# Decayed linear attention and two MLPs: the order of a chunk's attention products, old state first instead of alternating by pairs of heads

## The chip, the core and the metric

The kernel runs on one core of one Trainium2 chip. The metric is the device time of one execution in microseconds (us). Three executions of the kernel before took 604.82, 605.13 and 610.63 us; the median is 605.13.

## What is computed

Attention over 2 batches, 8 heads, 768 tokens and 64 features a head, with a decay per head instead of a softmax, and then two MLPs of 512 to 2048 to 512 on the 1536 tokens. The reference, cut:

```python
for b in range(nb):                                        # attention, block by block
    intra = einsum('bhic,bhjc->bhij', qb, kb) * Dmask      # scores, decayed and causal
    intra = einsum('bhij,bhjd->bhid', intra, vb)           # values
    inter = einsum('bhid,bhde->bhie', qb * lam_pow, kv_state)   # old state
    out[:, :, sl] = intra + inter
    kv_state = lam_block * kv_state + einsum('bhsd,bhse->bhde', kb * rev_pow, vb)
h = x @ w_in;  x = (h * clip(h + 3, 0, 6) / 6) @ w_out     # first MLP
h = relu(x @ w_in2);  out = (h * h) @ w_out2               # second MLP
```

## The kernel before

The attention is done in 12 chunks of 128 tokens, 6 for each batch. The MLPs work on three blocks of 4 chunks (512 tokens). All products are float32. The weights arrive as float64 and are turned into two float32r parts each ("decoding", lines 144 to 191) mostly on VectorE, 64 pieces of 512 numbers a partition. Decoding steps are handed out by `fill` and `weight` between the other steps of VectorE.

For one chunk the attention has these parts; the names are those of the tiles in the trace.

- Scores (`scores`, L286): `psc`, keys by queries, for the first block with a block diagonal query (L295, full array), for later chunks one product for each head with 64 rows (L305). The eight heads of a chunk lie in two PSUM tiles, one for each half t of the rows. VectorE multiplies them with the decay into `A` (L299, L307).
- New state (`state_values`, L316): `pst`, eight products of the decayed keys `kd` and the values, 128 rows by 64 columns of the array. VectorE makes the new state `kv` of it and of `kvs`, the old state decayed by GpSimd (L323, L326). The last chunk of a batch (5 and 11) has none.
- The chunk's output (`state_values`): `px` in this text, `pxt` in the trace, one PSUM tile. To every head belong an old-state product (L334: 64 rows by 64 columns, of `kv_old` and the decayed query `qs`) and a values product (L337: 128 rows by 64 columns, of `v` and `A`), which is added to it. The first chunk of a batch (0 and 6) has no old state. ScalarE copies the sum into `xh` (L339) and VectorE takes the rest into `xl` (L342).
- GpSimd makes `kd` and `qs` for the next chunk in `prepare` (L272, L280, L282). `kd` and `qs` have one buffer each, so `qs` of the next chunk can be made only when the last old-state product of this chunk has read the buffer, and `kd` when the last new-state product has.

An old-state or values product of one head (64 by 128 outputs in float32) stands in the trace as two matmul records; so eight products are a group of 16 records. The words F, S, N, O and V stand below for the big products of the MLPs (`ph` L358, `py` L395), the scores of later chunks, the new state, the old state and the values.

Chunks 0 to 3 are done first, with seven PSUM buffers (the stage up to 34.4 us). From there on chunks 4 to 11 are spread through the first MLP's work, and all their PSUM tiles (`psc` twice, `pst`, `pxt`) share a pool `ps_a` of two buffers, handed out in turn: scores take both, then the two tiles of `state_values`, then the next scores. A tile waits until the tile two places before it has been read. The order on every engine is set by a scheduler that may put big products between the parts of a chunk; TensorE then runs its list in that order and waits at the first instruction that isn't ready. The attention ends at 107 us; nothing behind it differs.

Of the kernel before, what the change touches and what calls it, by code (L numbers as in the profile page):

```python
# [8 lines left out]
F32 = mybir.dt.float32  # L9
# [5 lines left out]
ALU = mybir.AluOpType  # L15
PSUM = bass.MemoryType.PSUM

P = 128
BLOCKS = (4, 4, 4)  # token blocks, in chunks of 128
WBUFS = {"wi": 5, "wo": 7}  # chunks of weights held as hi and lo  # L20
WARM = 10
RAW = 4  # loads of weights under way
GROUP = 4  # chunks of 128 hidden units that are summed in PSUM
# us of decoding given to VectorE after each part of a unit of work
FILL = {"s": 0.8, "h1": 1.0, "h2": 0.8, "y": 1.6, "a": 1.0}


# [1 line left out]
def decay_attention_moe_moe(  # L29
# [10 lines left out]
    w_out2: bass.AP,  # L40
    out: bass.AP,
):
    """Decayed linear attention and two MLPs.

    The weights are float64, given as int64 of the same bits. A weight, and every other
    operand of the large products, is held as the sum of two float32r numbers (hi of 12
    significant bits and lo of the rest); hi*hi + hi*lo + lo*hi has float32's accuracy.
    Activations stay transposed, [feature, token], up to the last product.

    lam: [128, head] the same in every row, then [head of a pair (64 rows each), pair]  # L50
    qT, kT: [chunk of 128 tokens, (head of a pair, feature), (pair, token)]
    k, v: [chunk, token, (head, feature)]
    w_in: [chunk of 128 hidden units, feature in its chunk, (chunk of features, unit, word)]
    w_out: [chunk of 128 hidden units, unit, (feature, word)]
    """
    nc = tc.nc
    NC = qT.shape[0]
    NP = lam.shape[1] // 3
    H = 2 * NP
    D = k.shape[2] // H  # L60
# [13 lines left out]

    halves = [slice(D * t, D * (t + 1)) for t in range(2)]

    # ---------------------------------------------------------------- loads
    # The first block's chunks borrow the sums' place; their queries lie block diagonal, so
    # that their products fill the array and bring TensorE's clock up.
    kT_t, k_t, q_t, v_t = {}, {}, {}, {}  # L80
    n_first = min(BLOCKS[0], 4)

# [27 lines left out]
        nc.sync.dma_start(out=k_t[c], in_=k[c])  # L110
        nc.sync.dma_start(out=v_t[c], in_=v[c])

    # ------------------------------------------------------- float64 weights
    keys = []
    n_ahead = WBUFS["wo"] - GROUP
    for i in range(2 * NF // GROUP):
# [4 lines left out]
        keys += [("wo", *x) for x in (fs[n_ahead:] if i else fs)]  # L121
    n_loaded, n_begun = 0, 0
    raw_t, abs_t, w_t = {}, {}, {}
    n_done = {"wi": 0, "wo": 0}  # weights that have had their last use
    pieces = []

    def load_ahead(n):
# [7 lines left out]
            n_loaded += 1  # L135

    def magnitude(n):
        """The exponent's lower eight bits become float32's."""
        if n < len(keys) and n not in abs_t:
            load_ahead(n + 1)  # L140
            abs_t[n] = dec.tile([P, DM], F32, tag="a", name="da")
            nc.scalar.activation(abs_t[n], raw_t[n][:, :, 1].bitcast(F32), AF.Abs, scale=2.0**16)  # L142

    def decode_steps(n):
        """Turns 512 float64 of every partition into hi and lo."""
        key = keys[n]
        kind = key[0]
        magnitude(n)
        t, a = raw_t.pop(n), abs_t.pop(n)
        lo32, hi32 = t[:, :, 0], t[:, :, 1]  # L150
        ai = a.bitcast(I32)
        u = dec.tile([P, DM], I32, tag="u", name="du")
        hi = wsp.tile([P, DM], F32R, tag=kind + "h", name=kind + "h", bufs=WBUFS[kind])
        lo = wsp.tile([P, DM], F32R, tag=kind + "l", name=kind + "l", bufs=WBUFS[kind])

        def clamp():
            # Under 2^-126: 0; from 2^128: inf.
            nc.vector.tensor_scalar(a, a, 2.0, 1.875 * 2.0**32, op0=ALU.max, op1=ALU.min)
            magnitude(n + 1)

        def shift():
            nc.vector.tensor_scalar(
                ai, ai, 4, 1, op0=ALU.logical_shift_left, op1=ALU.logical_shift_right
            )

        def join():
            # u: the value cut to 21 significant bits.
            nc.vector.scalar_tensor_tensor(  # L168
                u, hi32, -(2**31), ai, op0=ALU.bitwise_and, op1=ALU.bitwise_or
            )  # L170
            nc.scalar.copy(hi, u.bitcast(F32))  # L171

        def power():
            # a: sign and power of two.
            nc.vector.tensor_scalar(ai, u, -(2**23), None, op0=ALU.bitwise_and)

        def lower():
            # a: what the lower word stands for.
            nc.vector.scalar_tensor_tensor(  # L179
                a, lo32.bitcast(U32), 2.0**-52, a, op0=ALU.mult, op1=ALU.mult  # L180
            )

        def rest():
            nc.vector.tensor_tensor(u.bitcast(F32), u.bitcast(F32), hi.bitcast(F32), op=ALU.subtract)  # L184

        def add():
            nc.vector.tensor_tensor(lo, u.bitcast(F32), a, op=ALU.add)  # L187
            w_t[key] = (hi, lo)
            load_ahead(n + 1 + RAW)

        return [(0.34, clamp), (0.34, shift), (0.6, join), (0.34, power), (0.6, lower), (0.6, rest), (0.6, add)]
# [28 lines left out]
            assert decode_piece()  # L220
        return w_t[key]

    # ------------------------------------------------------------ constants
    ident = const.tile([P, P], F32, name="ident")
    lams = const.tile([P, H + NP], F32, name="lams")
    lam_h, lam_p = lams[:, :H], lams[:, H:]
# [22 lines left out]
                op0=ALU.mult, op1=ALU.add,  # L249
            )  # L250

    # ------------------------------------------------------------ attention
    blk_of = {}
    first_tok = []
    c0 = 0
# [28 lines left out]
                )  # L284

    def scores(c, pool):  # L286
        """Keys by queries of a chunk, all heads, decayed and causal."""
        A_t[c] = ap.tile([P, NP, 2, P], F32, tag="A", name="A")
        if c < n_first:
            for half in range(2):  # L290
# [16 lines left out]
            nc.vector.tensor_tensor(A_t[c][:, :, t, :], ps[t], decay[:, :, t, :], op=ALU.mult)  # L307

    def state_values(c, pool):
        """The state after a chunk, and the chunk's part of x, transposed."""  # L310
        first, last = c % CPB == 0, c % CPB == CPB - 1
        kv_old, kv_new = kv[(c + 1) % 2], kv[c % 2]
        if not last:
            ps = pool.tile([P, NP, D], F32, tag="at", name="pst")
            for h in range(H):
                nc.tensor.matmul(  # L316
                    ps[halves[h % 2], h // 2, :], kd_t[c][:, h, :], v_t[c][:, h * D : (h + 1) * D], start=True, stop=True
                )
            if first:
                nc.vector.tensor_copy(kv_new, ps)  # L320
            else:
                kvs = ap.tile([P, NP, D], F32, tag="kvs", name="kvs", bufs=1)
                nc.gpsimd.tensor_tensor(  # L323
                    kvs, kv_old, lpow[:, :, P - 1 : P].to_broadcast([P, NP, D]), op=ALU.mult
                )
                nc.vector.tensor_tensor(kv_new, ps, kvs, op=ALU.add)  # L326
        j, i = blk_of[c]
        if j not in x_hi:
            x_hi[j], x_lo[j] = x_tiles(j)
        ps = pool.tile([P, NP, P], F32, tag="at", name="pxt")  # L330
        for a in range(NP):
            if not first:
                for r in halves:
                    nc.tensor.matmul(ps[r, a, :], kv_old[r, a, :], qs_t[c][r, a, :], start=True, stop=False)  # L334
            for t, r in enumerate(halves):
                h = 2 * a + t
                nc.tensor.matmul(ps[r, a, :], v_t[c][:, h * D : (h + 1) * D], A_t[c][:, a, t, :], start=first, stop=True)  # L337
        dst = slice(i * P, (i + 1) * P)
        nc.scalar.copy(x_hi[j][:, :, dst], ps)  # L339
        if c + 1 < NC:  # L340
            prepare(c + 1)
        nc.vector.tensor_tensor(  # L342
            x_lo[j][:, :, dst], ps, x_hi[j][:, :, dst].bitcast(F32), op=ALU.subtract
        )
        if c < 2 or c >= n_first:
            load_chunk(c + (n_first if c < 2 else 2))

    # ----------------------------------------------------------------- mlps
    g_t, acc, y_new = {}, {}, {}

    def hidden(layer, j, f):
        """128 hidden units of a block of tokens, split into hi and lo."""
        n = BLOCKS[j] * P
        wih, wil = weight(("wi", layer, f))
        ph = ps_h.tile([P, n], F32, tag="ph", name="ph")
# [22 lines left out]
        fill(FILL["h2"])  # L378

    def project(layer, j, grp, e):  # L380
        """Adds one tile's products over a group of hidden units to its sum."""
        n = BLOCKS[j] * P
        w = n if layer == 0 else DM
        es = slice(e * P, (e + 1) * P)
# [35 lines left out]
            nc.sync.dma_start(out=out[r0 : r0 + P, :], in_=t)  # L420
        fill(FILL["y"])

    # ------------------------------------------------------------- schedule
    idle = const.tile([P, 512], BF16, name="idle")
    nc.vector.memset(idle, 0.0)
    setup()
    n0 = BLOCKS[0]
    with tc.tile_pool(name="ps_a0", bufs=7, space=PSUM) as ps_a0:
        # Products of zeros raise TensorE's clock while the first loads are under way.
        warm = ps_a0.tile([P, 512], F32, tag="warm", name="warm", bufs=1)  # L430
        for _ in range(WARM):
            nc.tensor.matmul(warm, idle[:, :P], idle, start=True, stop=True)
# [33 lines left out]
    l, g, j = seq[-1]  # L466
    units += [("y", l, j, g, e) for e in range(ny(l, j))]

    # steps of attention that may be left when a unit starts
    x_first = {}  # L470
    for i, u in enumerate(units):
        if u[0] == "y" and u[1] == 0:
# [58 lines left out]
```

## Time and profile before

| what | value |
|---|---|
| runs | 604.82, 605.13, 610.63 us |
| the profiled execution: its span, first to last instruction | 603.6 us |
| the profile names no time of its own for that execution; median of the runs less the span | 1.5 us |
| matmul busy share of the span (PE) | 98% |
| VectorE (DVE) busy share | 69% |
| granted TensorE clock | 1.00, throughout |

PE is TensorE's matmuls, PEld its weight loads, DVE VectorE, ACT ScalarE, POOL GpSimd. Durations of matmuls overlap, so the distance from one start to the next says what a product costs; in a timeline a row has a start, the length from its first start to its last end, and the count of records.

### The profile page before, as it was taken

The numbers are of one execution on the slowest core, as the hardware profiler recorded it, in microseconds if no ns is written. First come the engines' busy times: TensorE is split into PE (matmuls) and PEld (weight loads), VectorE is DVE, ScalarE is ACT, GpSimd is POOL, SyncE is SP. The second block draws the span as 40 slices with busy tenths as digits, with TensorE's granted clock in tenths as the row PEclk, the third lists the DMA queues.
The fourth block names the chain that finished last, engine by engine and source line by source line (L and its number), as shares of the span: only waits on it lengthen the run. The fifth ranks groups of instructions, "written<-read, shape, count | busy, mean of one in ns | idle before, by whom it ended". The sixth has DMA issues, their size and how long they took to land.

```text
span 603.6 us, 7743 instructions
## 1 busy us (share of the span) xinstructions
PE 591.7 (98%) x2986; PEld 472.4 (78%) x2986; DVE 415.7 (69%) x739; ACT 254.8 (42%) x417; POOL 39.1 (6%) x43
## 2 busy tenths in 40 slices
PE   6989999999999999999999999999999999999997
PEld 3656666788888888888888888888888888888885
DVE  8978989377966897588977893459457875532222
ACT  2134234264442353245445566457326634523421
POOL 5722232000000000000000000000000000000000
PEclk9999999999999999999999999999999999999999
DMA  8945642212321223111311241012101110001011
GB/s 261 379 128 210 184 149 89 71 35 71 104 71 35 71 71 104 36 38 68 103 37 35 71 138 37 35 71 104 71 35 71 61 45 0 1 0 53 18 71 70
DMA packets 19637, 49.79 MB, mean 82 GB/s; under 512 B 2192, under 2 KB 4240, under 8 KB 19600
## 3 DMA queue, kind: packets, MB, share of 16 engines
q1 hardware_dynamic: 19600, 49.30, 24.0%
q8 instruction: 23, 0.38, 0.3%
q14 instruction: 14, 0.11, 0.1%
HBM read 46.14 MB, written 3.15 MB: 82 GB/s over the span
## 4 chain that ended last, share of the span: by engine, by line
PE 96%; DMA 2%; SPq 1%; DVE 1%; ACT 0%; issue 0%; POOL 0%; POOLq 0%; ACTq 0%
PE py L395 44%; PE ph L358 44%; PE pxt L337 3%; PE pxt L334 3%; PE psc L305 2%; PE pst L316 1%; DMA kT<-in_kT 1%; DMA lent<-in_qT 1%; PE psc L295 1%; SPq L104 0%; POOL qs L280 0%; DVE xl L342 0%; ACT r L369 0%; DVE acc L404 0%; DVE g L370 0%
## 5 line engine op out<-in xcount | busy, mean ns | idle before, releaser
L358 PE MATMUL ph<-xh,wih 128*128 128x512 f32 x384 | 150.6, 392 | 1.4 <-DVE xl L342 1.4
L358 PE MATMUL ph<-xh,wil 128*128 128x512 f32 x384 | 149.8, 390 | 0.0
L358 PE MATMUL ph<-xl,wih 128*128 128x512 f32 x384 | 149.5, 389 | 0.0
L376 DVE TENSOR_TENSOR gl<-g,gh 128x512 fp32r<-128x512 f32 x96 | 66.0, 687 | 65.0 <-ACT gh L374 64.4
L358 PEld LDWEIGHTS ph<-xh,wih 128*128 128x128 f32 x384 | 72.1, 188 | 17.5 <-DVE xl L342 1.7
L358 PEld LDWEIGHTS ph<-xh,wil 128*128 128x128 f32 x384 | 72.1, 188 | 15.4 <-issue 0.3
L358 PEld LDWEIGHTS ph<-xl,wih 128*128 128x128 f32 x384 | 72.1, 188 | 14.6
L404 DVE TENSOR_TENSOR acc<-acc,py 128x512 f32<-128x512 f32 x72 | 49.2, 683 | 47.9 <-PE py L395 47.2
L395 PE MATMUL py<-gh,woh 128*128 128x512 f32 x192 | 75.2, 392 | 0.0
L395 PE MATMUL py<-gl,woh 128*128 128x512 f32 x192 | 74.8, 391 | 0.0
L395 PE MATMUL py<-woh,gh 128*128 128x512 f32 x192 | 74.8, 390 | 0.0
L395 PE MATMUL py<-woh,gl 128*128 128x512 f32 x192 | 74.7, 389 | 0.0
L395 PE MATMUL py<-wol,gh 128*128 128x512 f32 x192 | 74.7, 389 | 0.0
L395 PE MATMUL py<-gh,wol 128*128 128x512 f32 x192 | 74.7, 392 | 0.0
L374 ACT CAST gh<-g 128x512 fp32r<-128x512 f32 x96 | 59.7, 622 | 33.0 <-DVE g L370 31.6
L142 ACT ACTIVATE da<-raw 128x512 f32<-128x512 f32 x64 | 42.8, 674 | 44.0 <-DVE wil L187 20.0
L372 ACT ACTIVATE r<-ph 128x512 f32<-128x512 f32 x48 | 28.6, 596 | 60.3 <-PE ph L358 60.0
L168 DVE SCALAR_TENSOR_TENSOR du<-raw,da 128x512 int32<-128x512 int32 x64 | 45.9, 717 | 0.7
L369 ACT ACTIVATE r<-ph,three 128x512 f32<-128x512 f32 x48 | 33.0, 687 | 30.7 <-PE ph L358 30.4
L184 DVE TENSOR_TENSOR du<-du,wih 128x512 f32<-128x512 f32 x32 | 22.8, 713 | 33.2 <-ACT wih L171 33.2
L179 DVE SCALAR_TENSOR_TENSOR da<-raw,da 128x512 f32<-128x512 uint32 x64 | 44.0, 687 | 0.6
L171 ACT CAST wih<-du 128x512 fp32r<-128x512 f32 x32 | 19.8, 620 | 55.5 <-PE ph L358 49.7
(66 smaller groups left out, 676.0 us busy)
## 6 DMA issues: line engine op xcount, KB each, us to landing
raw<-in_w_in SPq DMA_DIRECT2D x32, 512.0 KB, 3.3
raw<-in_w_out SPq DMA_DIRECT2D x32, 512.0 KB, 3.3
out<-acc SPq DMA_DIRECT2D x12, 256.0 KB, 2.0
kT<-in_kT SPq DMA_DIRECT2D x10, 256.0 KB, 3.6
k<-in_k SPq DMA_DIRECT2D x10, 256.0 KB, 3.4
v<-in_v SPq DMA_DIRECT2D x10, 256.0 KB, 2.8
q<-in_qT SPq DMA_DIRECT2D x8, 256.0 KB, 3.7
lent<-in_qT SPq DMA_DIRECT2D x8, 128.0 KB, 5.5
```

The lines of the kernel that those rows point to most:

```text
L142: nc.scalar.activation(abs_t[n], raw_t[n][:, :, 1].bitcast(F32), AF.Abs, scale=2.0**16)
L168: nc.vector.scalar_tensor_tensor(u, hi32, -(2**31), ai, op0=ALU.bitwise_and, op1=ALU.bitwise_or)
L171: nc.scalar.copy(hi, u.bitcast(F32))
L179: nc.vector.scalar_tensor_tensor(a, lo32.bitcast(U32), 2.0**-52, a, op0=ALU.mult, op1=ALU.mult)
L184: nc.vector.tensor_tensor(u.bitcast(F32), u.bitcast(F32), hi.bitcast(F32), op=ALU.subtract)
L358: nc.tensor.matmul(ph, w[:, a * P : (a + 1) * P], x[:, a, :], start=a == 0 and i == 0, stop=a == KD - 1 and i == 2,)
L369: nc.scalar.activation(r, ph, AF.Relu, bias=three)
L372: nc.scalar.activation(r, ph, AF.Relu)
L374: nc.scalar.copy(gh, g)
L376: nc.vector.tensor_tensor(gl, g, gh.bitcast(F32), op=ALU.subtract)
L395: nc.tensor.matmul(py, a, b, start=f == fs[0] and i == 0, stop=f == fs[-1] and i == 2)
L404: nc.vector.tensor_tensor(t, t, py, op=ALU.add)
```

## The change

In `state_values` the tile of the chunk's output is taken first, and all eight old-state products are issued into it; then come the new state's products, and then all eight values products. The flag that clears what the bank holds is set on the first pair alone, where before each pair set its own. The count of products is the same. Comments were taken out as well, and so line numbers move: L334 is L320 after, L316 is L326, L323 is L333, L337 is L343, L358 is L367 and L395 is L404.

```diff
     def state_values(c, pool):
         first, last = c % CPB == 0, c % CPB == CPB - 1
         kv_old, kv_new = kv[(c + 1) % 2], kv[c % 2]
+        px = pool.tile([P, NP, P], F32, tag="at", name="pxt")
+        if not first:
+            for a in range(NP):
+                for r in halves:
+                    nc.tensor.matmul(
+                        px[r, a, :], kv_old[r, a, :], qs_t[c][r, a, :], start=a == 0, stop=False, skip_group_check=True
+                    )
         if not last:
             ps = pool.tile([P, NP, D], F32, tag="at", name="pst")
...
-        ps = pool.tile([P, NP, P], F32, tag="at", name="pxt")
         for a in range(NP):
-            if not first:
-                for r in halves:
-                    nc.tensor.matmul(ps[r, a, :], kv_old[r, a, :], qs_t[c][r, a, :], start=True, stop=False)
             for t, r in enumerate(halves):
                 h = 2 * a + t
-                nc.tensor.matmul(ps[r, a, :], v_t[c][:, h * D : (h + 1) * D], A_t[c][:, a, t, :], start=first, stop=True)
+                nc.tensor.matmul(
+                    px[r, a, :], v_t[c][:, h * D : (h + 1) * D], A_t[c][:, a, t, :],
+                    start=first and a == 0, stop=True, skip_group_check=True,
+                )
```

TensorE at chunk 4, before: the new state stands alone among the big products of the first block, and then the old state's and the values' products take turns.

```order
L358 MATMUL ph<-xl_203,wih 128x512
L316 MATMUL pst<-v,kd 64x64 x8
L358 MATMUL ph<-xh_202,wil 128x512
L358 MATMUL ph<-xh_202,wih 128x512
L358 MATMUL ph<-xl_203,wih 128x512
L334 MATMUL pxt<-qs,kv_83 64x128 x2
L337 MATMUL pxt<-A,v 64x128 x2
L334 MATMUL pxt<-qs,kv_83 64x128 x2
L337 MATMUL pxt<-A,v 64x128 x2
L334 MATMUL pxt<-qs,kv_83 64x128 x2
L337 MATMUL pxt<-A,v 64x128 x2
L334 MATMUL pxt<-qs,kv_83 64x128 x2
```

The same place of the changed kernel:

```order
L367 MATMUL ph<-xl_204,wih 128x512
L320 MATMUL pxt<-qs,kv_83 64x128 x8
L343 MATMUL pxt<-A,v 64x128
L326 MATMUL pst<-v,kd 64x64 x8
L343 MATMUL pxt<-A,v 64x128 x7
L367 MATMUL ph<-xh_203,wil 128x512
```

The chunk's products now stand in one piece, and three big products that stood between the new state and the rest have moved behind them.

TensorE behind chunk 7's values, before: three big products, then the scores of chunk 9 in two halves of four (one PSUM tile each) around one big product.

```order
L337 MATMUL pxt<-A,v 64x128 x2
L395 MATMUL py<-gh,wol 128x512
L395 MATMUL py<-gh,woh 128x512
L395 MATMUL py<-gl,woh 128x512
L305 MATMUL psc<-q,kT 128x128 x4
L395 MATMUL py<-gh,wol 128x512
L305 MATMUL psc<-q,kT 128x128 x4
```

The same place of the changed kernel:

```order
L343 MATMUL pxt<-A,v 64x128 x7
L404 MATMUL py<-gh,wol 128x512
L305 MATMUL psc<-q,kT 128x128
L404 MATMUL py<-gh,woh 128x512
L404 MATMUL py<-gl,woh 128x512
L305 MATMUL psc<-q,kT 128x128 x3
L404 MATMUL py<-gh,wol 128x512
L404 MATMUL py<-gh,woh 128x512
L404 MATMUL py<-gl,woh 128x512
L305 MATMUL psc<-q,kT 128x128 x4
```

The scores of chunk 9 now come one big product after the values, not three, and in three pieces.

GpSimd in the first stage, chunks 2 and 3, before:

```order
L272 TENSOR_TENSOR kd<-lent_93,decay 128x512
L323 TENSOR_TENSOR kvs<-kv_83,lpow 128x256
L280 TENSOR_TENSOR qs<-lent_92,lpow 64x512 x2
L272 TENSOR_TENSOR kd<-more,decay 128x512
L323 TENSOR_TENSOR kvs<-kv_82,lpow 128x256
L280 TENSOR_TENSOR qs<-lent_92,lpow 64x512 x2
```

The same place of the changed kernel:

```order
L280 TENSOR_TENSOR qs<-lent_92,lpow 64x512 x2
L272 TENSOR_TENSOR kd<-lent_93,decay 128x512
L333 TENSOR_TENSOR kvs<-kv_83,lpow 128x256
L280 TENSOR_TENSOR qs<-lent_92,lpow 64x512 x2
L272 TENSOR_TENSOR kd<-more,decay 128x512
L333 TENSOR_TENSOR kvs<-kv_82,lpow 128x256
```

Each chunk's decayed query has moved ahead of its decayed keys.

## Rows read from the trace of the kernel before

**Rows 1.** The page: busy us of each engine (share of the span) and instructions.

```profile
PE 591.7 (98%) x2986; PEld 472.4 (78%) x2986; DVE 415.7 (69%) x739; ACT 254.8 (42%) x417; POOL 39.1 (6%) x43
```

**Rows 2.** Stretches: length, then busy us of PE, PEld, DVE, ACT, POOL; clock, DMA, GB/s.

```profile
34.40:107.00 72.60, 72.06 (x581) 48.90 (x582) 66.13 (x118) 28.32 (x47) 17.25 (x15) 1.00 0.49 157
107.00:603.60 496.60, 492.88 (x2172) 406.98 (x2170) 322.19 (x572) 219.72 (x361) 0.00 (x0) 1.00 0.17 58
41.40:70.20 28.80, 28.71 (x241) 18.73 (x240) 25.66 (x46) 10.55 (x17) 9.16 (x8) 1.00 0.53 176
```

**Rows 3.** Timeline of TensorE, chunk 4's output among the big products.

```profile
41.25 0.39 PE L358 MATMUL ph<-xh,wih 128*128 128x512 f32 x1
41.48 0.40 PE L358 MATMUL ph<-xl,wih 128*128 128x512 f32 x1
41.81 0.43 PE L334 MATMUL pxt<-qs,kv 64*64 64x128 f32 x4
42.18 0.44 PE L337 MATMUL pxt<-A,v 128*64 128x128 f32 x4
...
44.75 0.50 PE L358 MATMUL ph<-xh,wil 128*128 128x512 f32 x1
45.09 0.40 PE L358 MATMUL ph<-xh,wih 128*128 128x512 f32 x1
```

**Rows 4.** Timeline of TensorE, groups that don't alternate and what follows them.

```profile
13.23 0.69 PE L316 MATMUL pst<-v,kd 128*64 128x64 f32 x16
13.74 1.04 PE L337 MATMUL pxt<-A,v 128*64 128x128 f32 x16
...
27.06 1.16 PE L305 MATMUL psc<-q,kT 64*128 64x128 f32 x16
28.15 0.69 PE L316 MATMUL pst<-more,kd 128*64 128x64 f32 x16
...
57.99 1.09 PE L337 MATMUL pxt<-A,v 128*64 128x128 f32 x16
59.02 0.50 PE L358 MATMUL ph<-xh,wih 128*128 128x512 f32 x1
...
59.91 1.16 PE L305 MATMUL psc<-q,kT 64*128 64x128 f32 x8
61.00 0.50 PE L395 MATMUL py<-gh,woh 128*128 128x512 f32 x1
```

**Rows 5.** Timeline of TensorE: chunk 1's start, chunk 3's output, the first big product.

```profile
17.60 0.69 PE L316 MATMUL pst<-v,kd 128*64 128x64 f32 x16
...
28.77 0.43 PE L334 MATMUL pxt<-qs,kv 64*64 64x128 f32 x2
30.03 0.43 PE L334 MATMUL pxt<-qs,kv 64*64 64x128 f32 x2 [0.84 <-POOL qs L280]
30.39 0.44 PE L337 MATMUL pxt<-A,more 128*64 128x128 f32 x4
...
34.45 0.50 PE L358 MATMUL ph<-xh,wih 128*128 128x512 f32 x1 [1.41 <-DVE xl L342]
```

**Rows 6.** Timeline of GpSimd in the first stage.

```profile
20.95 3.12 POOL L280 TENSOR_TENSOR qs<-lent,lpow 64x512 f32<-64x512 f32 x2 [0.43 <-PE pxt L334]
24.15 1.06 POOL L272 TENSOR_TENSOR kd<-more,decay 128x512 f32<-128x512 f32 x1
25.17 1.07 POOL L323 TENSOR_TENSOR kvs<-kv,lpow 128x256 f32<-128x256 f32 x1
```

**Rows 7.** Timeline of VectorE, chunk 5's second `A` to chunk 7's `xl`.

```profile
40.72 0.68 DVE L307 TENSOR_TENSOR A<-psc,decay 128x512 f32<-128x512 f32 x1
...
65.36 1.21 DVE L168 SCALAR_TENSOR_TENSOR du<-raw,da 128x512 int32<-128x512 int32 x1
...
69.51 0.69 DVE L342 TENSOR_TENSOR xl<-pxt,xh 128x512 fp32r<-128x512 f32 x1 [0.91 <-ACT xh L339]
```

More of the change, by code (lines that the diff above doesn't have):

```diff
@@ L329, in state_values @@
             x_hi[j], x_lo[j] = x_tiles(j)
-        ps = pool.tile([P, NP, P], F32, tag="at", name="pxt")
         for a in range(NP):
-            if not first:
-                for r in halves:
-                    nc.tensor.matmul(ps[r, a, :], kv_old[r, a, :], qs_t[c][r, a, :], start=True, stop=False)
             for t, r in enumerate(halves):
                 h = 2 * a + t
-                nc.tensor.matmul(ps[r, a, :], v_t[c][:, h * D : (h + 1) * D], A_t[c][:, a, t, :], start=first, stop=True)
+                nc.tensor.matmul(
+                    px[r, a, :], v_t[c][:, h * D : (h + 1) * D], A_t[c][:, a, t, :],
+                    start=first and a == 0, stop=True, skip_group_check=True,
+                )
         dst = slice(i * P, (i + 1) * P)
-        nc.scalar.copy(x_hi[j][:, :, dst], ps)
+        nc.scalar.copy(x_hi[j][:, :, dst], px)
         if c + 1 < NC:
@@ L342, in state_values @@
         nc.vector.tensor_tensor(
-            x_lo[j][:, :, dst], ps, x_hi[j][:, :, dst].bitcast(F32), op=ALU.subtract
+            x_lo[j][:, :, dst], px, x_hi[j][:, :, dst].bitcast(F32), op=ALU.subtract
         )
```

## The prediction

> **What bounds the kernel now.** I read the page's busy times first: PE is busy for 98% of the span, VectorE for 69% [rows 1]. So what counts is TensorE's own stream, and a wait on it. Then the table by stretches: from 34.4 to 107 us, where chunks 4 to 11 lie among the first MLP's products, PE is busy for all but 0.5 of 72.6 us, but VectorE is nearly so too, for 66.1 us [rows 2]. Behind 107 us VectorE has work for only 65% of the time, and the order there is unchanged. So the change is worth what PE saves before 107 us, as far as VectorE lets it. The timeline of TensorE gives the prices, and GpSimd's says what the first stage waits for.
>
> **The price of taking turns.** In chunk 4 an old-state group of 4 records (O) starts at 41.81, the values group (V) at 42.18, and eight such groups last until the big product (F) at 44.75: 2.94 us, 0.367 a group [rows 3]. Groups that don't alternate are cheaper. Sixteen V records take 1.03 us until the next product, 57.99 to 59.02. Sixteen new-state records (N) take 0.51 us when V follows, which uses the array in the same shape (128 rows, 64 columns), and 0.62 us when O follows (28.15, then 28.77 in the next group); scores (S) take 1.09 us before N [rows 4, 5]. So the change of shape costs about 0.11 us, and by the V groups (0.367 against a quarter of 1.03) 0.11 to 0.15.
>
> Sixteen O records in a row are not in the trace. One bound: both halves of the rows work at the same time, as in S, the nearest group; then 1.03 to 1.09, and I take 1.06. The other bound: one half after the other. One half alone takes 0.36 us (30.03 to 30.39, where its partner had run before a wait [rows 5]), about 0.25 of it without the change of shape; eight halves are then 2.0 us plus 0.11. The row that decides is near: a group with both halves takes 0.367, no more than one half, so the halves overlap. [...]
>
> **What TensorE saves, part by part.**
> - Ten chunks have an old state (1 to 5, 7 to 11). The output: 2.94 becomes 1.06 + 1.03, so −0.85 each, −8.5 us.
> - In chunks 1, 2, 3, 9 and 10 the new state stood before O and now stands before V: 0.62 becomes 0.51, together −0.55.
> - In chunks 4 and 7 the new state stood alone among F. Going in costs 0.10 (41.48 to 41.81 is 0.33, against 0.23 from one F to the next) and the F behind costs 0.11 more than usual (44.75 to 45.09 is 0.34 [rows 3]); 0.62 + 0.2 becomes 0.51: −0.31 each, −0.6.
> - In chunk 8 the order now cuts V in two around two F: one more visit, +0.35.
> - Scores: four products of one half of the rows alone take as long as eight of both (16 records from 27.06 to 28.15, 8 records from 59.91 to 61.00, both 1.09 [rows 4]). Chunk 10's scores were two such visits and become one (−0.75); chunk 9's go from two visits to three (+0.3); those of 7 and 11 now begin with two products of the same half (+0.25 each); those of 6 had waited within and lose 0.3. Sum −0.25.
>
> All of it is −9.55 us; chunks 1 to 3 hold −2.9 of that and the stretch behind 34.4 us the other −6.65.
>
> **The first stage.** Chunk 2's old state had waited 0.4 us and chunk 3's 1.25 us for GpSimd's `qs` (28.77 to 30.39 is 1.62, against 0.367 [rows 5]). GpSimd needs 3.1 us for `qs`, then 1.06 for `kd` and 1.07 for `kvs` [rows 6]: 5.2 us a chunk. Its order is now `qs`, `kd`, `kvs`, and `qs` may start when O, no longer V, is done. From chunk 1's products, which started at 17.6 [rows 5]: O ends at 18.7, `qs` for chunk 2 at 22.0, and TensorE comes to O of chunk 2 at 22.15, so without a wait. `qs` for chunk 3 then begins at 24.15, behind `kvs`, and ends at 27.3; TensorE has its scores done at 25.9 and waits 1.4 us. So waits of 1.65 go and 1.4 come. V of chunk 3 ends at about 29.95 instead of 33.05, and the first F starts at 31.35 instead of 34.45 [rows 5]: −3.1 us. VectorE's work, then without a gap, ends at 29.9 and just covers this.
>
> **Behind 34.4 us: VectorE takes some of it back.** The new order of tiles has a price. The output now takes the buffer of `ps_a` that the first half of the next scores but one reuses; so these scores wait at their first product for `xl`, the last thing that VectorE does for a chunk, where before the new state's buffer came first, and that was free early. The new state's products for their part wait for the second half of `A`, not the first. I went along both engines' orders with the durations of the rows, from the end of chunk 5's second `A`, which moves from 41.40 to 38.3. VectorE has 25.66 us of work from there to the end of chunk 7's `xl` at 70.20, and only 3.1 us idle [rows 2, 7]. TensorE would be 3.1 + 1.16 + 0.85 + 1.16, and some tenths for scores, about 6.3 us ahead at that place; VectorE started 3.1 ahead and can't make up the rest, for it also waits for TensorE's results three times. So the new waits on TensorE are: 0.3 us at the scores of chunk 6, 1.25 at the new state of chunk 6 (ready 51.1, `A` done 52.35), 0.95 at the scores of chunk 8, and 2.0 at those of chunk 9 (ready at 64.35; `xl` of chunk 7 done at 66.3). Before, none of these was above 0.15. Sum 4.4 us after rounding.
>
> Check by the lead at that last place: the scores of chunk 9 start at 66.35 instead of 69.68, but with 8 F of the second product done instead of 14; 6 × 0.23 is 1.4, so the lead is 1.9 us. Behind it I find no wait above 0.1: chunk 8 gives 0.5, the scores 0.2, chunks 9 and 10 0.96 each, chunk 11 0.85. That makes 3.5, and 5.4 together.
>
> **Sum.** −9.55 in products, −0.25 in the first stage's waits, +4.4 in new waits: −5.4 us. Against the profiled execution's span of 603.6 that is 598.2; with the 1.5 us that lie around it by the median, 605.1 − 5.4 = 599.7. A measurement of this kernel can tell about 1% from no change, that is 6.05 us, so this lies just inside "no change".
>
> **Rivals.**
> - VectorE is not in the way. For it: one of its decoding steps took 1.21 us there, while other steps on tiles of that size took 0.68 and 0.69 [rows 7], so some of its work is stretched and may be less so; and 3.1 us of idle time is nearly what is needed. Against it: 66.1 us of work for VectorE in 72.6 us [rows 2], which TensorE would then run through in 66. Then −9.8, 595.3. Chance 0.16.
> - VectorE costs more: it doesn't shorten its idle time at all, so the lead at chunk 9's scores is nearly 0, and only what comes behind is gained: −2 to −3.5, near 602.3. For it: each of its steps there waits for one of TensorE's or ScalarE's. Chance 0.15.
> - The change doesn't do what it says: O's halves don't overlap in a run of eight (the bound of 2.1 us). Each of ten chunks gives back 1.05 us, −9.8 becomes +0.7, and less waits remain to be added: about 605. Against it stands the 0.367. Chance 0.06. [...]
> - Slower: the output's buffer. If every one of the six later scores waits for `xl` as chunk 9's does, 2.0 us, and every one of the five new states for the second `A` as chunk 6's does, 1.25, that is 18 us of waits against 9.8 saved: about +8, 613. It is slower from a mean wait of 0.9 us at these eleven places. Against it: of VectorE's 6.5 idle us in that stretch about half lie behind 70 us [rows 2], and big products stand between these places in the new order. Chance 0.03.
>
> **How the numbers follow.** My forecast has 0.60, with its own range from −3.5 to −7.3 us; a third of it lies beyond −6.05. Faster by over 1%: 0.20 + 0.16 = 0.36. Slower by over 1%: 0.03. Within 1%: 0.61. The range leaves out half of the rival with −9.8, the no-overlap case and the slower one: 596.0 to 603.0.
>
> **What would show it right or wrong.** In the changed kernel's trace: 16 records of O in one row with the next start 1.03 to 1.09 us later (2.1 would show the overlap wrong); N followed by V after 0.51; the first F near 31.4 us; a wait of 1.0 to 1.5 us for `qs` at chunk 3; PE idle before the scores of chunks 8 and 9 with `xl` as the releaser; the last values of chunk 11 ending 5 to 6 us earlier than before, and from there on the same distances as before. If the end of the attention moves by more than 8 us, VectorE was not the limit; if the waits before `psc` are missing and the gain is still small, the price of alternating was read wrong.

## The result, and the profile after

The changed kernel took 600.9 us (median of 7 runs, 598.27 to 605.4), the kernel before 606.16 us (7 runs, 604.82 to 610.63). The ratio is 0.99, with an interval of 0.9864 to 0.9937 (the two medians alone give 0.991): about 1% faster, just short of what was called faster here. The forecast was 599.7, with a range of 596.0 to 603.0. The profiled execution has a span of 596.5 us against 603.6, both at a granted clock of 1.00.

The page and the table by stretches of the changed kernel, where [rows 1, 2] show the kernel before. The first stretch runs from the first big product to the first one behind the attention, the second from there to the end.

```profile
PE 582.0 (98%) x2986; PEld 473.7 (79%) x2986; DVE 419.0 (70%) x739; ACT 254.5 (43%) x417; POOL 41.4 (7%) x43
...
PE 87%; DVE 10%; DMA 1%; SPq 1%; issue 0%; ACT 0%; DVEq 0%
```

```profile
31.17:99.58 68.41, 66.36 (x581) 50.35 (x581) 67.67 (x117) 27.66 (x46) 19.82 (x16) 1.00 0.53 166
99.58:596.50 496.92, 493.24 (x2174) 407.43 (x2172) 323.24 (x574) 220.01 (x362) 0.00 (x0) 1.00 0.17 58
```

TensorE does the same 2986 products in 9.7 us less of busy time. In the stretch of the MLPs VectorE is now the busier of the two: 67.67 of 68.41 us. The page's chain of waits gives VectorE 10% of the span. Behind the attention nothing moved: 496.92 us here, 496.93 before (106.67 to 603.6).

TensorE's timeline of the changed kernel, in the places that answer to [rows 3 to 5]: chunk 1, chunk 3 up to the first big product, chunk 4, the scores of chunk 6, chunk 10.

```profile
14.98 1.97 PE L295 MATMUL psc<-lent,lent 128*128 128x256 f32 x8 [0.93 <-DMA lent<-in_qT]
16.88 1.09 PE L320 MATMUL pxt<-qs,kv 64*64 64x128 f32 x16
17.90 0.69 PE L326 MATMUL pst<-v,kd 128*64 128x64 f32 x16
18.41 1.05 PE L343 MATMUL pxt<-A,v 128*64 128x128 f32 x16
...
27.18 1.09 PE L320 MATMUL pxt<-qs,kv 64*64 64x128 f32 x16 [2.12 <-DVE kv L336]
...
31.17 0.50 PE L367 MATMUL ph<-xh,wih 128*128 128x512 f32 x1 [1.41 <-DVE xl L351]
...
38.14 0.43 PE L343 MATMUL pxt<-A,v 128*64 128x128 f32 x2
38.33 0.71 PE L326 MATMUL pst<-v,kd 128*64 128x64 f32 x16
38.84 1.04 PE L343 MATMUL pxt<-A,v 128*64 128x128 f32 x14
...
41.62 0.71 PE L305 MATMUL psc<-q,kT 64*128 64x128 f32 x4
42.98 1.15 PE L305 MATMUL psc<-q,kT 64*128 64x128 f32 x12 [0.65 <-DVE xl L351]
...
92.07 1.09 PE L320 MATMUL pxt<-qs,kv 64*64 64x128 f32 x16
93.09 0.69 PE L326 MATMUL pst<-v,kd 128*64 128x64 f32 x16
93.61 1.05 PE L343 MATMUL pxt<-A,v 128*64 128x128 f32 x16
```

Sixteen O records now take 1.02 us (92.07 to 93.09), N ahead of V 0.52, V about 1.0 until the next product. The new waits are two kinds: at 27.18 chunk 3's O waits 2.12 us for VectorE's state sum, and at 42.98 the scores of chunk 6 stop for 0.65 us after two of their eight products, for `xl`. The same stop is 0.44 us in chunk 7's scores and 0.47 in chunk 11's. At 37.12 chunk 4's O also waits 0.48 us for `A`.

The 7.1 us of the profiled span split into: −0.73 before chunk 2's scores (they start at 14.98 instead of 15.71; their queries came earlier from memory); −2.55 from there to the first big product (18.74 became 16.19); −3.81 from there to the end of the attention (72.22 became 68.41); −0.01 behind it.

For the stretch from chunk 5's scores to the first big product behind the attention I added up the distances from one start to the next by kind of product, with the waits that rows name apart (us):

| kernel | O and V | N | S | F, 120 of them | waits | sum |
|---|---|---|---|---|---|---|
| before | 21.62 | 3.81 | 11.43 | 32.03 | 0.38 | 69.27 |
| changed | 15.80 | 3.48 | 12.43 | 31.71 | 2.04 | 65.46 |
| difference | −5.82 | −0.33 | +1.00 | −0.32 | +1.66 | −3.81 |

So the grouping gave what it should (5.82 us), and scores cut in two and new waits took 2.66 of it back.

### The profile page after: what moved, and what is told of

Its sections match the earlier page's. It is cut to its first block, busy times and chain, and to the rows that moved or that the text cites. A ratio compares the mean times of both kernels' runs of the same rounds, so it can differ in the third digit from the quotient of the medians.

```text
span 596.5 us, 7747 instructions
## 1 busy us (share of the span) xinstructions
PE 582.0 (98%) x2986; PEld 473.7 (79%) x2986; DVE 419.0 (70%) x739; ACT 254.5 (43%) x417; POOL 41.4 (7%) x43
## 4 chain that ended last, share of the span: by engine, by line
PE 87%; DVE 10%; DMA 1%; SPq 1%; issue 0%; ACT 0%; DVEq 0%
PE py L404 42%; PE ph L367 42%; DVE du L184 1%; DVE da L179 1%; DVE du L168 1%; DVE da L158 1%; DVE da L175 1%; DVE xl L351 1%; DVE A L307 1%; DMA lent<-in_qT 1%; PE psc L305 1%; PE pxt L320 1%; PE pxt L343 1%; DVE A L299 1%; DVE wol L187 1%; DVE da L162 1%
## 5 line engine op out<-in xcount | busy, mean ns | idle before, releaser
L367 PE MATMUL ph<-xh,wih 128*128 128x512 f32 x384 | 150.5, 392 | 1.4 <-DVE xl L351 1.4
L367 PE MATMUL ph<-xh,wil 128*128 128x512 f32 x384 | 150.0, 391 | 0.0
L367 PE MATMUL ph<-xl,wih 128*128 128x512 f32 x384 | 149.8, 390 | 0.0
L367 PEld LDWEIGHTS ph<-xh,wih 128*128 128x128 f32 x384 | 72.1, 188 | 17.2 <-DVE xl L351 1.7
L367 PEld LDWEIGHTS ph<-xh,wil 128*128 128x128 f32 x384 | 72.1, 188 | 15.3 <-issue 0.3
L367 PEld LDWEIGHTS ph<-xl,wih 128*128 128x128 f32 x384 | 72.1, 188 | 14.9 <-issue 0.2
L404 PE MATMUL py<-gh,woh 128*128 128x512 f32 x192 | 75.4, 393 | 0.0
L404 PE MATMUL py<-gh,wol 128*128 128x512 f32 x192 | 75.0, 393 | 0.0
L404 PE MATMUL py<-woh,gh 128*128 128x512 f32 x192 | 74.9, 390 | 0.0
L404 PE MATMUL py<-gl,woh 128*128 128x512 f32 x192 | 74.9, 390 | 0.0
L404 PE MATMUL py<-woh,gl 128*128 128x512 f32 x192 | 74.8, 390 | 0.0
L404 PE MATMUL py<-wol,gh 128*128 128x512 f32 x192 | 74.8, 389 | 0.0
```

The lines of the kernel that those rows point to most:

```text
L367: nc.tensor.matmul(ph, w[:, a * P : (a + 1) * P], x[:, a, :], start=a == 0 and i == 0, stop=a == KD - 1 and i == 2,)
L404: nc.tensor.matmul(py, a, b, start=f == fs[0] and i == 0, stop=f == fs[-1] and i == 2)
```

## The experiments

Four theories were open. A: each change of the array's shape costs 0.11 to 0.15 us, and that alone is what alternating cost. B: instead, a values product waits for the old-state product that it adds to. C: the stops in the scores are for a PSUM buffer. D: VectorE is the next limit, so a removed wait comes back behind it. "The stretch" below is that of the table above; the stretches quoted ran at a granted clock of 0.99 to 1.00, but for the first 2.5 us of the one of N, V, O (0.85).

**The order of before, but no values product right behind the sum it adds to.**

```diff
         for a in range(NP):
             old(a)                  # pair a's old-state products
-            val(a)                  # pair a's values products
+            val((a + 2) % NP)
```

> TensorE's list is that of the kernel before, group by group; only the values products of another pair of heads (two further on) follow each old-state pair, so no product adds to what the one just before it wrote. Theory A (each change of the array's shape costs 0.11 to 0.15 us): the groups stay 0.36 to 0.37 us apart, the output of a chunk 2.9 us, and the time is that of before within 0.3%. Theory B (a product waits for the sum that it adds to): groups 0.25 to 0.27 apart, an output 2.1 us, and 5 to 8 us less than before.

606.34 us (604.81 to 611.16), ratio 0.9983 [0.9949, 1.0017]; the stretch 69.26 us against 69.27. TensorE's timeline of this run, chunk 4:

```profile
44.39 0.44 PE L336 MATMUL pxt<-qs,kv 64*64 64x128 f32 x4
44.76 0.44 PE L345 MATMUL pxt<-A,v 128*64 128x128 f32 x4
45.13 0.44 PE L336 MATMUL pxt<-qs,kv 64*64 64x128 f32 x4
45.49 0.44 PE L345 MATMUL pxt<-A,v 128*64 128x128 f32 x4
```

The groups still start 0.37 us apart, though none follows the group it adds to. B falls.

**Two pairs at a time: four runs of one shape a chunk, where before has eight and the changed kernel two.**

```diff
+        for b in range(0, NP, 2):
+            for a in range(b, b + 2):
+                old(a)
+            for a in range(b, b + 2):
+                val(a)
```

> New state first, then the output by two pairs at a time: the four old-state half products of two pairs, the four value products of the same two pairs, and the same for the other two. Per chunk four runs of one shape stand where before has eight and the changed kernel two. A (each change of shape costs about 0.14 us, as (2.94 - 2.09) / 6 of the output's time says): the output costs about 2.09 + 2 x 0.14 = 2.4 us, the seven chunks of the MLP stretch (chunk 5's scores to the first large product behind the attention) come to 69.3 - 7 x 0.57 + 0.5 to 1.4 of waits = 65.8 to 66.7 us, and the whole to 604 to 605. The rival (only products of all pairs in one run are fast, because the next weights are loaded ahead within a run): nothing for half a run, output near 2.9 us, stretch near 69, whole at 605 to 606.

605.04 us (604.25 to 606.64), ratio 0.9956 [0.9926, 0.9986]; the stretch 67.13 us, 0.4 above what was expected. TensorE's timeline, chunk 4:

```profile
43.20 0.65 PE L336 MATMUL pxt<-qs,kv 64*64 64x128 f32 x8
43.79 0.66 PE L345 MATMUL pxt<-A,v 128*64 128x128 f32 x8
44.37 0.65 PE L336 MATMUL pxt<-qs,kv 64*64 64x128 f32 x8
44.96 0.66 PE L345 MATMUL pxt<-A,v 128*64 128x128 f32 x8
45.55 0.50 PE L383 MATMUL ph<-xh,wil 128*128 128x512 f32 x1
```

The output costs 2.35 us here (43.20 to 45.55), 2.94 with eight runs and 2.05 with two (chunk 11 of the changed kernel, 97.53 to 99.58): 0.15 us for each run fewer, both from eight to four and from four to two. A holds, with its size, and the rival (2.9 us) falls. That the stretch came out above the forecast is the scores again: 12.23 us of them against 11.43 before.

**Grouped as in the change, but with the new state first: N, O, V and N, V, O.**

```diff
+        new_state()
+        for a in range(NP): old(a)
+        for a in range(NP): val(a)      # e3: these two lines the other way round
```

> The new state first, as before, then all old-state and then all values products. Theory A: an output of 2.05 us in place of 2.94 in ten chunks, so TensorE has 8.9 us less to do before 107 us. If the waits for xl at the scores of chunks 6, 7 and 11 come from the old state's place ahead of the new state's (theory C), they aren't here, and the time is 6 to 8.5 us below before, so 0 to 2.5 below the changed kernel. If VectorE limits whatever the order (theory D), waits for it come up elsewhere and the gain is 5 to 6.5 us, that of the changed kernel.

> New state, then values, then old state. The same number of changes of shape as in the changed kernel, and the old state has 1.5 us more of cover for kv and qs: the wait of 2.1 us before chunk 3's old state falls below 1 us. Theory C: 7 to 9.5 us below before. Theory D: 5 to 6.5, like the changed kernel.

N, O, V: 604.8 us (602.13 to 608.27), ratio 0.9952 [0.9918, 0.9986]. N, V, O: 603.93 (601.52 to 606.13), ratio 0.9923 [0.9893, 0.9953]. Their stretches, 65.72 and 65.80 us, are the changed kernel's 65.46 within 0.4: there grouping counts, and the order of the three groups hardly. The first stage is where they lose. TensorE waits there 3.0 and 2.7 us for GpSimd's `qs`, where the changed kernel waits for none. For N, V, O I had expected less than 1 us of that; it was wrong. So were all the expectations for the whole: by the ratios the runs are 2.9 and 4.7 us below before, where 5 or more had been expected. The stops at the scores of chunks 7 and 11 are gone, as C has it, but that of chunk 6 is not (0.55 and 0.54 us for `xl`), and waits for `A` have come up (1.2 and 1.3 us).

**A third buffer for the attention, taken from the hidden sums: in the changed kernel, and as a control in the kernel before. And one taken from the projection sums.**

```diff
-    ps_h = ... name="ps_h", bufs=3
-    ps_a = ... name="ps_a", bufs=2
+    ps_h = ... name="ps_h", bufs=2
+    ps_a = ... name="ps_a", bufs=3
```

> The changed kernel with three PSUM buffers for attention and two, not three, for the sums of the hidden units. If the scores of chunks 6, 7 and 11 wait for a buffer (theory C), these waits go, 3 us: 9 us below before, 3 below the changed kernel. If VectorE limits (theory D), the waits move to another place and the time stays within 1 us of the changed kernel. If two buffers are too few for the hidden units, TensorE waits at ph and it is slower than the changed kernel by up to 0.5 us for each of 24 units near the attention.

> The kernel before with one buffer moved from the hidden sums (3 to 2) to the attention's (2 to 3), nothing else. It tells whether the 2.8 us that the changed kernel gained from these buffers in the stretch of the MLPs is the changed order's wait taken away (C) or something that any order would have gained. C: before has no score product that waits longer than 0.3 us for a buffer outside chunks 8 to 10 (scores there in pieces), so its stretch goes from 69.3 to 67.5 to 69.3 us and the part behind the attention rises by the same 1.3 us as there; whole 604 to 607. Rival (the buffers shorten everything, the order has little in it): the stretch goes to 66.5 or less and the whole to 603.5 or less.

> The changed kernel with the third buffer for the attention taken from the projection sums (3 to 2) where the experiment on the banks took it from the hidden sums. C: the three waits of the scores (0.65, 0.44, 0.47 us, and 3.1 us with what the split costs) go, the stretch of the MLPs comes to 62.4 to 63.2 us as there; whether the whole gains depends on what a projection sum waits with two buffers: its four product groups of an output tile last about 2.6 us and the sum on VectorE has to be done by then. Without such waits 597.5 to 599; if each of some 60 projections waits 0.1 to 0.5 us, 604 to 625.

| kernel | median (range), us | ratio to before | stretch | behind it |
|---|---|---|---|---|
| before | | | 69.27 | 496.93 |
| before, third buffer | 603.57 (601.98 to 608.4) | 0.9954 [0.9914, 0.9994] | 66.96 | 496.85 |
| changed | 600.9 (598.27 to 605.4) | 0.99 [0.9864, 0.9937] | 65.46 | 496.92 |
| changed, third buffer | 601.39 (598.78 to 604.93) | 0.9898 [0.9848, 0.9947] | 62.68 | 498.21 |
| changed, third buffer from `ps_y` | 601.61 (600.2 to 602.34) | 0.9888 [0.983, 0.9947] | 62.73 | 498.2 |

The waits for `xl` at the scores are gone, and so are the scores in pieces: 8.73 us of S instead of 12.43. C holds. But the control's stretch gained 2.31 us too, more than C allowed it (1.8 at most) and less than its rival (2.8 at least). Its scores fell from 11.43 to 8.45 us without a wait that rows had named: with two buffers the scheduler had already cut them into halves. So most of what this buffer gives, any order would have got; grouping is worth 3.81 us with two buffers and 4.28 with three.

TensorE's waits from 33 to 105 us in the changed kernel with the third buffer show what is late next:

```profile
PE pxt L343 <- DVE A L307: 1.5, 1, 1.5
...
PE pst L326 <- DVE A L307: 0.8, 2, 0.4
PE py L404 <- ACT woh L171: 0.7, 1, 0.7
```

All three are work on which VectorE's pace tells: `A` is its own, and the weight `woh` comes from its decoding by way of ScalarE. Together they are 2.97 us in place of 2.04. Another 1.3 us comes back right behind the attention, where a projection now waits 1.25 us for hidden values; that is the 498.2. It is not the price of the buffer taken from the hidden sums: the run that takes it from `ps_y` has the same wait, and the control has none, though C had expected 1.3 us there for it as well. The medians didn't move against the changed kernel; with the buffer from `ps_y` 597.5 to 599 had been expected.

**Half the decoding between the steps of the first stage.**

```diff
-FILL = {"s": 0.8, ...
+FILL = {"s": 0.4, ...
```

> The changed kernel with half the decoding that is put on VectorE between the steps of the first stage (0.8 to 0.4 us after each), nothing else. It tells what the old-state products of chunk 3 wait for there (2.1 us until the state sum is done). D (VectorE's decoding stands ahead of the state sum): the wait falls to 0.6 to 1.4 us, what is left being the scaled queries of GpSimd, the first stage from 16.2 to 15 to 15.7 us; the decoding left out has to be done later and may show as waits of large products for weights (up to 3 us). Rival (GpSimd's queries or the product chain set it): the wait stays within 0.3 of 2.1 us or goes over to the queries at the same length. Whole: 599 to 602.

600.42 us (599.14 to 604.3), ratio 0.9902 [0.987, 0.9933]. The wait at chunk 3's O is 2.12 us, to the digit that of the changed kernel, as the rival has it. But the edit had not reached the place: the scheduler still put the same three steps of decoding ahead of that state sum. The run says nothing on the question, and the next one asks it again. Its stretch is 64.47 us, 1.0 shorter than the changed kernel's: of the three stops at the scores only that of chunk 6 (0.66 us) is left. Why the other two are gone was not followed up.

**One decoding step tied behind chunk 2's state sum.** The copied column is overwritten at once; it only gives that step something to wait for.

```diff
         def power():
+            if n == 1:
+                nc.vector.tensor_copy(a[:, :1], kv[0][:, 0, :1])
             nc.vector.tensor_scalar(ai, u, -(2**23), None, op0=ALU.bitwise_and)
```

> The changed kernel with one copy of a single column (of the state after chunk 2 into a place that the next step overwrites), by which the decoding of the second weight tile stands behind that state's sum on VectorE instead of three steps of it ahead (1.17 + 0.67 + 1.75 us there). It tells what chunk 3's old-state products waited 2.1 us for. D (VectorE's decoding): the sum ends 1 to 3 us sooner, the products then wait only for GpSimd's scaled queries, which ended 0.9 us before the sum did: the wait falls from 2.1 to 0.9 to 1.4 us and the stretch from chunk 2's scores to the first large product from 16.2 to 15.0 to 15.6 us where the clock stays at its upper level. Rival (the queries, or GpSimd's scaled old state, set it): the wait stays within 0.3 us of 2.1. Whole: 599 to 601, since the decoding put back may come late for the second hidden tile (up to 1 us).

601.89 us (598.21 to 604.45), ratio 0.9891 [0.9857, 0.9926]. VectorE's timeline of the changed kernel shows what stood ahead of the sum (26.62), and GpSimd's when the scaled queries were done (23.08 + 3.07, so 26.15):

```profile
23.16 1.27 DVE L299 TENSOR_TENSOR A<-psc,decay 128x512 f32<-128x512 f32 x2
24.36 0.67 DVE L179 SCALAR_TENSOR_TENSOR da<-raw,da 128x512 f32<-128x512 uint32 x1
24.95 1.75 DVE L184 TENSOR_TENSOR du<-du,wih 128x512 f32<-128x512 f32 x1
26.62 0.41 DVE L336 TENSOR_TENSOR kv<-pst,kvs 128x256 f32<-128x256 f32 x1
```

```profile
23.08 3.07 POOL L280 TENSOR_TENSOR qs<-lent,lpow 64x512 f32<-64x512 f32 x2
```

With the tie the sum stands straight behind `A`, and chunk 3's O did not wait for it any more. TensorE's timeline of this run, chunk 3 and the first F:

```profile
27.76 1.57 PE L321 MATMUL pxt<-qs,kv 64*64 64x128 f32 x16
...
29.96 1.05 PE L344 MATMUL pxt<-A,more 128*64 128x128 f32 x16
34.98 0.80 PE L368 MATMUL ph<-xh,wih 128*128 128x512 f32 x1 [3.97 <-DVE xl L352]
```

Counted from chunk 2's scores (17.34), V of chunk 3 starts 12.62 us later, 1.12 sooner than in the changed kernel. But the first F starts 17.64 us later where 15.0 to 15.6 had been expected and the changed kernel has 16.19: the wait is now 3.97 us for `xl`, and VectorE was busy for 13.89 of the 14 us from 20 to 34. The clock was 0.81 from 11 to 20 us and 1.00 from 20 to 28 us. From chunk 2's scores to the next product it is 1.93 us, against 1.90 in the changed kernel at 1.00, so the low lay ahead of those scores; and VectorE came to chunk 2's state sum 9.52 us behind them, 1.27 later than in the next run; whether the one comes from the other is not shown. The next run has the same edit and a clock of 1.00 all along the first stage.

**Both: the tie and the third buffer.**

> The kernel of the run before together with the third attention buffer from the hidden sums, as the best version of what the runs have shown. C and D: the first stage as there, the stretch of the MLPs at 62 to 63.5 us in place of 65.5, and behind it the 1.25 us wait for VectorE again (a projection that waits for the hidden values), so 1 to 2.5 us less than the changed kernel: 598 to 600.5. Rival (VectorE already sets the pace, so that what one wait gives, another takes): within 0.7 us of the changed kernel, 600 to 602.

600.78 us (596.96 to 601.95), ratio 0.9881 [0.983, 0.9933]; the profiled execution has a span of 595.2 and a clock of 1.00 in the first stage and the stretch. Its timelines of TensorE and VectorE:

```profile
24.41 1.16 PE L306 MATMUL psc<-q,kT 64*128 64x128 f32 x16
25.50 0.43 PE L321 MATMUL pxt<-qs,kv 64*64 64x128 f32 x2
26.13 1.08 PE L321 MATMUL pxt<-qs,kv 64*64 64x128 f32 x14 [0.20 <-POOL qs L281]
27.59 0.69 PE L327 MATMUL pst<-more,kd 128*64 128x64 f32 x16 [0.38 <-POOL kd L273]
28.11 1.04 PE L344 MATMUL pxt<-A,more 128*64 128x128 f32 x16
31.34 0.50 PE L368 MATMUL ph<-xh,wih 128*128 128x512 f32 x1 [2.18 <-DVE xl L352]
...
103.54 0.50 PE L405 MATMUL py<-gh,woh 128*128 128x512 f32 x1 [1.25 <-ACT gh L384]
```

```profile
23.72 0.42 DVE L337 TENSOR_TENSOR kv<-pst,kvs 128x256 f32<-128x256 f32 x1
...
28.01 1.28 DVE L308 TENSOR_TENSOR A<-psc,decay 128x512 f32<-128x512 f32 x2
29.21 1.14 DVE L188 TENSOR_TENSOR wil<-du,da 128x512 fp32r<-128x512 f32 x1
30.27 0.41 DVE L337 TENSOR_TENSOR kv<-pst,kvs 128x256 f32<-128x256 f32 x1
30.61 0.68 DVE L352 TENSOR_TENSOR xl<-pxt,xh 128x512 fp32r<-128x512 f32 x1
```

Chunk 3's O waits 0.20 us instead of 2.12: its cause was VectorE's decoding ahead of the sum. Counted from chunk 2's scores (15.47 here, 14.98 in the changed kernel), V of chunk 3 starts 1.10 us sooner (12.64 against 13.74) but the first F only 0.32 sooner (15.87 against 16.19). The decoding put back (29.21) now stands ahead of `xl`, and F waits 2.18 us for that instead of 1.41. For the first stage D holds: VectorE's list decides when it ends, and a wait taken away at one place came back at the next.

This is the fastest version the runs have, but only just. In profiled executions at a clock of 0.999 it took 596.96 us and the changed kernel 598.27; at 0.994 it took 599.39 against 599.89 to 601.52, and at 0.990 to 0.991 601.4 to 601.95 against 603.0. The medians (600.78, 600.9), of executions at mixed clocks, don't tell them apart. The stretch is 62.70 us, as expected; the whole is 0.3 above its forecast and where the rival had it.

**Ten products without use in the waits of the first stage.** They are added to the version above, six around chunk 0's scores and four ahead of the first F.

> The version of the run before with ten extra large products whose result nobody reads, in two waits of the first stage: six around chunk 0's scores (TensorE stood idle there for 3 to 5 us) and four between chunk 3's values and the first large product (idle for 1.4 to 4 us). It asks what the low granted clock hangs on that some executions show between 11 and 40 us (0.5 to 0.85) and others don't. If it follows TensorE's idle time before it: no executions at a mean clock under 0.995, the times within 1.5 us of each other at 597 to 599, and the profile at 1.00 in each stretch of the first stage. If it has nothing to do with it: the same spread as before, mean clock from 0.987 to 1.0, median 600 to 602.5. Where the clock stays up, the extra products themselves should cost under 0.7 us, for they stand in waits.

599.77 us (597.48 to 604.21, 6 runs), ratio 0.9872 [0.9829, 0.9914], with mean clocks of 0.993 to 0.997. The profile still shows 0.81 from 11 to 20 us, behind a wait of 4.27 us for queries from memory. From 20 to 60 us it shows 1.00, and a new low of 0.79 from 68 to 72 and 0.78 from 72 to 76 us, where TensorE had waited 0.93 us for a weight after 2.47 us for `A` at 58. Neither expectation came out: the clock still fell, and the lowest means (under 0.993) did not show, which with 6 runs may be chance. Inconclusive.

## Why the prediction came out right, point by point

- **The price of taking turns** was read correctly: 0.11 to 0.15 us a change by the rows of before, 0.15 by three numbers of runs in a chunk. The rival in which O's halves don't overlap (605 us) fell with O's 1.02 us, forecast as 1.06, where one half after the other was estimated at 2.1. So the two row halves, which write other partitions of one tile, work side by side here.
- **What TensorE saves:** for the seven outputs of the stretch −5.95 was forecast (0.85 each; −5.60 with the V of chunk 8 cut in two) and O and V gave −5.82. N ahead of V took 0.51 to 0.52 in chunks 1 and 10, as forecast. Chunk 4 gave less than its 0.31: the pair of V records ahead of N costs 0.19 (38.14 to 38.33).
- **The first stage** was to give 3.1 us and gave 2.55. The step "TensorE has its scores done at 25.9 and waits 1.4 us" for GpSimd's `qs` was 0.7 us too small and had the cause wrong. GpSimd was done at 26.15, and VectorE's state sum at 27.03 was what O waited 2.12 us for. That sum had been left out of the working, because in the kernel before N stood ahead of the outputs and the sum was early: it ended at 25.07, and chunk 3's O began at 28.77.

```profile
24.66 0.41 DVE L326 TENSOR_TENSOR kv<-pst,kvs 128x256 f32<-128x256 f32 x1
```

- **The new waits** are the step that failed: "the output now takes the buffer of `ps_a` that the first half of the next scores but one reuses". The three stops come at the third product. The list of chunk 6's scores begins with two products of the first half, which ran; the third, of the second half, waited for `xl`. So the first half still gets the new state's buffer, and the two buffers are not handed out in turn, which the description ahead of the prediction had said. The forecast waits (1.25 at chunk 6's new state, 0.95 and 2.0 at the scores of chunks 8 and 9) did not occur; 0.65 (forecast 0.3), 0.44 and 0.47 did at the scores of chunks 6, 7 and 11, and 0.48 at chunk 4's O.
- **Their size** was too high. With the scores (−0.25 + 4.4) the stretch was to give back 4.15 us; it gave back 2.66. A stop of 0.65 costs 1.36 (41.62 to 42.98), since the two products ahead of it run alone, and the six behind it take 1.09 us (42.98 to 44.07), as long as all eight would. The stretch gave −3.81 where −2.25 was forecast.
- **The sum** without the earlier queries is −6.4 us against −5.4: 0.55 too much in the first stage, 1.56 too little behind it. The two errors had opposite signs, which is luck. So is that the medians differ by 5.3 us, so near to the forecast: the profiled spans differ by 7.1, and executions at an equal clock by about 6.6 (last section).
- **VectorE in the way** was the reason given for a small gain. In the first stage that held: the wait taken from chunk 3's O came back at the first F. In the stretch it held only in part. With a third buffer and the same work for VectorE the stretch fell by another 2.78 us, so much of what it had given back was the price of two shared buffers. VectorE's part there is the new waits (2.97 us for 2.04) and the 1.3 us that came back behind the attention. The rival without VectorE in the way (−9.8) stayed far off.

## What to carry to other kernels

Where small products of two array shapes alternate, count the changes of shape and price one from a place in the trace where the same products stand alone; grouping is then worth the number of changes times that (here 0.15 us), without regard to which product adds to which (0.37 us a group in either order here). Before the sum is believed, ask which engine was just behind TensorE. Here VectorE had 6.5 us idle in the stretch and TensorE's busy time fell by 9.7 us in all; a wait removed in the first stage came back, all but 0.3 us, at the next tile that VectorE had to make. And a pool of two PSUM buffers shared by four tiles decides the order of the products as much as the code does: in the stretch a third buffer was worth 2.3 us to the old order and 2.8 to the new one, of which 1.3 came back right behind it.

## What the runs showed of the hardware that was not expected

The granted clock is not the same in all executions of one kernel. The profiles of the kernel before and of the changed one show 1.00 all along; the profile of the N, V, O order shows this in the first stage (stretch, its length, busy us of PE, PEld, DVE, ACT and POOL, then the clock):

```profile
11.00:20.00 9.00, 8.20 (x80) 6.70 (x80) 6.72 (x12) 1.78 (x3) 5.08 (x5) 0.81 1.08 337
20.00:28.00 8.00, 8.00 (x122) 6.71 (x120) 7.93 (x12) 1.79 (x3) 6.56 (x6) 1.00 1.02 399
28.00:34.00 6.00, 1.94 (x24) 1.22 (x20) 5.17 (x8) 1.27 (x3) 5.85 (x6) 0.95 0.42 149
34.00:40.00 6.00, 5.91 (x16) 4.29 (x18) 4.11 (x9) 1.38 (x3) 0.50 (x1) 0.50 0.48 156
```

From 34 to 40 us the granted clock was 0.50, behind 6 us in which TensorE was busy for only 1.94; there the first big products stood 0.43 us apart instead of 0.23. The 0.81 of the first row follows a wait of 4.0 us for queries from memory. The length of the wait there alone doesn't decide: from 11 to 20 us the clock was 1.00 behind a wait of 3.56 us (half the decoding) and 0.66 behind one of 2.74 (two pairs at a time). In the stretches read from 40 to 107 us, of 20 us and more, all profiles but one are at 0.99 to 1.00; the exception is the run with the added products, with the low of 68 to 76 us told there. The clock moves the time about as much as the change does, by 5 to 7 us. Executions of the kernel before took 604.2 to 606.3 us at a mean clock of 1.0 and 609.6 to 611.8 at 0.988 to 0.989; those of the changed kernel 598.27 at 0.999, 599.89 to 601.52 at 0.994 and 605.4 at 0.986. At an equal clock of 0.994 before took 607.04 and 607.61, so the change is worth about 6.6 us there, and a median of few runs can shift with the clocks they met. Why executions of the same kernel meet different clocks, no run here shows.

Most of VectorE's decoding steps, whose tiles all lie in SBUF, took longer while GpSimd worked. From the timelines of the changed kernel:

```profile
34.49 0.69 DVE L184 TENSOR_TENSOR du<-du,wih 128x512 f32<-128x512 f32 x1
```

The same step took 1.75 us at 24.95, while GpSimd made `qs`. In the first 110 us of the kernel before and of the changed one, these steps took 0.41 to 0.43 or 0.67 to 0.69 us (by the step) where GpSimd did nothing. Of those for more than half of which it worked, 16 of 19 before and 20 of 31 after took longer than that by more than 0.03 us, up to 1.51 and 1.75 us. The steps that read a PSUM tile (`A`, `kv`, `xl`) took 0.67 to 0.69 or 0.41 to 0.42 us beside GpSimd too. So part of what VectorE's list costs the first stage comes with GpSimd's work there; no run tried to move that work.
